# A fused attention and two-MoE kernel: squares to ScalarE, y of two chunks transposed on TensorE, and a new hand-written order of the lead and the first block

## Chip, cores and metric

The kernel runs on one NeuronCore of a Trainium2 chip. The metric is the device time of one execution in microseconds (us). The kernel before takes 1087.73 us in the median of three runs (1086.11, 1087.73 and 1088.6).

## What is computed

Three layers follow each other, all in float32 at the interface.

```python
# 1. attention-like recurrence, B, H, S, D = 4, 8, 768, 48
mag = sqrt(a_re**2 + a_im**2)
scale = minimum(mag, 0.999) / (mag + 1e-6)      # a is shortened to a magnitude below 1
for t in range(S):                              # per batch and head, state S is D x D, complex
    S = a[t][:, None] * S + outer(k[t], v[t])
    y[t] = q[t] @ real(S)
x = y as (B*S, H*D) = (3072, 384)
# 2. first MoE-like layer, w_in 384 x 2048, w_out 2048 x 384
h = x @ w_in;  x = (h * tanh(softplus(h))) @ w_out        # "mish"
# 3. second layer, w_a and w_b 384 x 1536, w_out 1536 x 384
out = ((x @ w_a) * (x @ w_b)) @ w_out
```

## The kernel before

The sequence is cut into chunks of 128 tokens: chunk c is sequence block j = c // 4 of batch b = c % 4, 24 chunks in all. Inside a chunk the recurrence becomes matrix products: decays are turned into logarithms and angles, summed along the tokens by a matmul with a triangular matrix, q and k are scaled and rotated by them, transposed on TensorE, multiplied with each other to scores, and the scores with v to y. What reaches a chunk from earlier blocks comes through a state matrix W per batch. The tokens of four chunks (one block, 512 tokens) then go through the first layer in 16 units of 128 hidden columns each, and after all blocks through the second layer in 12 units per block. The layers work on pairs of tensors (a high part and a low part in the TensorE format fp32r), three matmuls for each product; the second product of block 0 is done in plain fp32 instead.

The names of steps that matter below, with their lines:

- decay steps of a chunk: `sq` squares the real and imaginary parts (decay_1, L283: on VectorE in L285 for chunks 1 to 3, on ScalarE in L287 otherwise), `add` sums them (L291), `ln`, `ex`, `tan`, `ell` follow; `pl` and `pt` are the running sums on TensorE (L355); `red` reduces the angle on VectorE (L386 to L388); `sin` is the trigonometry on ScalarE; `rq` and `rk` rotate q and k (L433), `tq`, `tk` transpose them on TensorE (L452), `s` makes scores on TensorE (psc, L475), `cp` masks them into SBUF on VectorE (L481).
- y of a chunk: chunks 0 and 1 are named in BY_MEMORY (L487) and make y already transposed (py, L508); ScalarE makes a high part (yh, L521), VectorE a low part (yl, L526), both are stored to DRAM by SyncE (L533) and loaded again as the layer's input (xh, xl, L590). Chunks 2 and 3 make y with tokens on the partitions (pyt, L498), ScalarE copies it out (yt), TensorE transposes it (px, L586), ScalarE makes the high part xh (L592) and VectorE the low part xl (L598).
- state: `ou` is the outer product of k and v on TensorE (pu, L552), with the pads of k cleared first by GpSimd (L547); `st` makes the state W from it on VectorE (L569).
- weights of the first layer: `w.n` loads 768 KB, `da`, `dc`, `db` split it in three passes of VectorE (L172, L174, L176), `hi` on ScalarE and `lo` on GpSimd (L188) make the two parts.
- first layer, unit n: `h.n` is the first product (hps, L650), `mn` (L656, VectorE), `ma`, `mb` (ScalarE) and `pr` (L680, VectorE) make mish, `x.n` is the second product into one PSUM accumulator (x2ps, L706).

The order of all this is no loop: up to the 17th unit of block 0 a string of step names is executed one by one in `run` (L969 to L997), and `in_order` pins what each of the five engines gets in exactly that order. Everything behind the list is placed by a planner that spreads attention steps over slots between the layer's units. `close` in the list ends the SBUF pools of the first four chunks (end_lead, L954); `open` ends their PSUM pool and opens the accumulator x2ps in its place (end_first, L959), so the first x2ps matmul has to wait until all that was in that PSUM pool (pl, pt, pyt, px and pu of the first four chunks) is read out.

Of the kernel before, what the change touches and what calls it, by code (L numbers as in the profile page):

```python
# [21 lines left out]
def kernel(  # L22
# [14 lines left out]
    nc = tc.nc  # L37
# [26 lines left out]
    B, H, S, D = q.shape  # L64
# [153 lines left out]
    st = {}  # L218
# [740 lines left out]
    def end_first():  # L959
# [9 lines left out]
    run("""  # L969
            a0 sq0 add0 ln0 ex0 a3 sq3 add3 tan0 at0 pt0 ell0 pl0 ln3 ex3 w.1 da.1 dc.1 db.1 hi.1 lo.1 a1 sq1  # L970
            tan3 add1 ell3 ep0 red0 ln1 he0 qk0 sc0 a2 sq2 v0 ex1 ell1 pl1 w.2 da.2 w.3 add2 dc.2 sin0 rq0
            tq00 tq10 tan1 da.3 rk0 dc.3 ht0 db.2 ln2 a4 qk1 re0 ep1 ex2 at1 he1 at3 cq10 sq4 tk10 ck10 pt1
            db.3 tan2 cq00 at2 hi.3 tk00 ck00 lo.3 sc1 add4 ln4 ell2 pl3 s10 cp10 pt3 pl2 ep2 red3 red1 pt2
            red2 he2 s00 cp00 py0 ep3 ex4 tan4 at4 qk2 qk3 sc2 ell4 pl4 v3 cy4 ca4 vm4 a5 w.4 v1 w.5 sin1 rq1
            tq11 rk1 pt4 tk11 sc3 sin2 rq2 ep4 he4 em4 qk4 sq5 cq11 yt0 he3 add5 tq12 cq12 tk01 ck01 ck11 ln5
            ou0 tq01 cq01 ex5 sin3 ht3 v2 red4 ht4 gm4 re4 re3 v4 re1 xl0 da.4 rk2 da.5 s11 cp11 dc.4 tq02
            cq02 s01 tk02 ou1 cp01 ck02 ht1 tk12 ck12 dc.5 sin4 py1 rq3 tq13 cq13 sy0 yt1 rk3 db.5 hi.5 db.4
            s02 cp02 xl1 st0 gm5 tk13 tq03 ck13 tk03 s12 cp12 st1 io0 re2 lo.5 s13 cp13 cq03 ck03 s03 py2 yt2
            cp03 py3 ht2 px2 xh2 yt3 ou3 sc4 tan5 at5 ell5 rk4 tk04 ms4 ck04 w.6 sy1 vm5 da.6 rq4 xl2 dc.6 px3
            xh3 xl3 close cy5 w.7 ca5 da.7 dc.7 db.7 tk14 ck14 pl5 ep5 tq14 cq14 tq04 ou2 io1 h.0 h.1 st3 mn.0  # L980
            st2 open so.0 sl.0 so.1 em5 db.6 s14 cp14 mn.1 cq04 hi.7 lo.7 ma.0 mb.0 pr.0 pt5 red5 a6 he5 re5
            qk5 w.8 v5 s04 cp04 ma.1 sq6 mb.1 add6 ln6 ou4 ex6 h.2 da.8 mn.2 pr.1 so.2 ma.2 mb.2 tan6 sc5 dc.8
            ell6 pr.2 x.0 x.1 sl.1 py4 sd4 ht5 sin5 ms5 at6 h.3 rk5 rq5 mn.3 ma.3 mb.3 yt4 db.8 h.4 mn.4 ma.4
            mb.4 w.9 da.9 cy6 ca6 pr.3 xl4 dc.9 db.9 tq05 cq05 x.2 pt6 red6 st4 x.3 sl.2 vm6 hi.9 lo.9 gm6
            tk15 w.10 a7 qk6 tq15 sq7 ck15 h.5 tk05 pr.4 da.10 mn.5 cq15 s15 cp15 ck05 ma.5 pl6 ep6 add7 dc.10
            db.10 s05 cp05 em6 mb.5 pr.5 h.6 so.3 ou5 ln7 ex7 ht6 sin6 w.11 sc6 he6 da.11 ell7 sy4 re6 py5
            tan7 dc.11 sd5 st5 v6 vm7 gm7 ms6 x.4 x.5 sl.3 mn.6 yt5 xl5 at7 ma.6 db.11 hi.11 lo.11 pl7 ep7 cy7
            w.12 ca7 pt7 h.7 rq6 rk6 tk16 mb.6 pr.6 h.8 em7 mn.7 ma.7 mb.7 red7 da.12 he7 w.13 re7 x.6 mn.8
            da.13 ma.8 tq06 pr.7 x.7 so.4 sl.4 tk06 dc.13 db.13 hi.13 lo.13 ck16 tq16 h.9 dc.12 db.12 mb.8
            pr.8 qk7 mn.9 ht7 cq06 ms7 cq16 s16 sin7 sc7 rq7 cp16 w.14 da.14 a8 dc.14 h.10 mn.10 ck06 s06 cp06  # L990
            ma.9 x.8 ou6 w.15 da.15 mb.9 pr.9 db.14 rk7 ma.10 mb.10 sy5 py6 yt6 sd6 so.5 so.6 x.9 sl.5 tq17
            cq17 tk17 ck17 dc.15 pr.10 xl6 w.16 da.16 dc.16 db.16 tq07 sq8 db.15 tk07 h.11 ck07 h.12 add8
            mn.11 mn.12 cq07 s07 cp07 qk8 v7 ou7 s17 cp17 hi.15 lo.15 ma.11 mb.11 x.10 ln8 pr.11 ex8 ell8 ph8
            py7 sd7 st7 ma.12 mb.12 sy6 cy8 io4 yt7 io6 h.13 mn.13 x.11 sl.6 pd8 pr.12 pl8 tan8 xl7 ma.13
            mb.13 pr.13 h.14 mn.14 h.15 at8 ca8 qh8 qd8 ma.14 mb.14 x.12 x.13 mn.15 ma.15 mb.15 pr.14 pr.15 a9
            sy7 io5 io7 h.16 h.17 mn.16 mn.17 ma.16 mb.16 pr.16 ma.17 mb.17 x.14 x.15 pr.17 st6
    """)  # L997
    last, after_lead = in_order(first, (E.DVE, E.Activation, E.PE, E.Pool, E.SP)), traced()
    slot[0] = 50
# [249 lines left out]
```

## Time and profile before

| | us |
|---|---|
| median of three runs | 1087.73 |
| the profiled execution, its own time | 1088.15 |
| its span from the first to the last instruction | 1086.40 |
| TensorE busy | 1044.8 (96%) |
| VectorE busy | 653.2 (60%) |
| ScalarE busy | 609.2 (56%) |
| GpSimd busy | 230.3 (21%) |

So 1.75 us of the profiled execution lie outside its span. The page gives the core's mean granted TensorE clock as 0.996 of full speed. In its 40 slices TensorE is at 2 tenths in the first slice of 27 us and at 8 in the second; from then on it is at 9 or more up to the last slice, with 7. VectorE's slices go the other way: 7, 9, 8, 8, 8, 7 at the start and 2 to 4 at the end. Lines and names in the profile are those of the kernel's source; "x2ps<-gh,wout" reads: x2ps is written from gh and wout.

### The profile page before, as it was taken

What the parts mean: (1) busy time and instruction counts of PE and PEld (TensorE: products, weight loads), DVE (VectorE), ACT (ScalarE), POOL (GpSimd) and SP (SyncE); (2) the same over time, 40 slices, a digit from 0 to 9 for tenths busy, and PEclk for the clock granted to TensorE, in tenths of its full rate; (3) what the DMA queues carried; (4) which work ended last, traced back from release to release, by engine and by line L of the source; (5) the groups of instructions that cost most, each with busy time, mean ns of one, the idle gap of its engine ahead of it and who ended that gap; (6) DMA issues with size and microseconds to landing.
All of it is one profiled execution on the core that took longest, in us unless ns stands there. A gap on an engine that the chain in (4) does not pass through costs nothing.

```text
span 1086.4 us, 15900 instructions
## 1 busy us (share of the span) xinstructions
PE 1044.8 (96%) x6054; PEld 871.9 (80%) x6054; DVE 653.2 (60%) x1001; ACT 609.2 (56%) x963; POOL 230.3 (21%) x265
## 2 busy tenths in 40 slices
PE   2899999999999999999999999999999999999997
PEld 1676676788888888888877788888888888888886
DVE  7988875888777777677579998632322422422222
ACT  7968877898788887898767842221122222212211
POOL 3022323444344344333231123100000000000000
PEclk9999999999999999999999999999999999999999
DMA  9665653444443344333155366110100100100000
GB/s 217 140 172 128 168 133 102 119 94 101 101 91 68 67 96 85 84 96 80 30 169 180 124 220 215 45 51 1 30 30 1 59 1 1 44 1 1 30 1 32
DMA packets 206813, 92.50 MB, mean 85 GB/s; under 512 B 144973, under 2 KB 191114, under 8 KB 206730
## 3 DMA queue, kind: packets, MB, share of 16 engines
q1 hardware_dynamic: 205674, 91.20, 34.0%
q8 instruction: 50, 0.82, 0.3%
q10 hardware_dynamic: 1056, 0.21, 0.1%
q14 instruction: 33, 0.27, 0.1%
HBM read 73.23 MB, written 18.15 MB: 84 GB/s over the span
## 4 chain that ended last, share of the span: by engine, by line
PE 80%; DVE 8%; ACT 6%; issue 2%; DMA 2%; POOL 1%; SPq 0%; ACTq 0%; DVEq 0%; POOLq 0%
PE ops L790 14%; PE x2ps L706 14%; PE psa L765 14%; PE psb L765 14%; PE hps L650 13%; PE psc L475 3%; ACT m L59 3%; PE py L508 3%; PE pkT L452 2%; PE pqT L452 1%; PE pu L552 1%; ACT L54 1%; DMA a<-in_a_im_dram 1%; DVE wf L174 1%; PE pt L355 1%
## 5 line engine op out<-in xcount | busy, mean ns | idle before, releaser
L776 DVE TENSOR_TENSOR a_sb<-a_sb,psb 128x512 f32<-128x512 f32 x72 | 49.4, 686 | 225.8 <-PE psb L765 225.8
L59 ACT ACTIVATE m<-m 128x512 f32<-128x512 f32 x192 | 118.9, 632 | 60.2 <-DVE m L656 55.0
L59 ACT ACTIVATE a_sb<-psa 128x512 f32<-128x512 f32 x72 | 43.0, 598 | 163.5 <-PE psa L765 161.4
L59 ACT ACTIVATE ph<-a_sb 128x512 fp32r<-128x512 f32 x72 | 45.4, 631 | 154.8 <-DVE a_sb L776 154.8
L650 PE MATMUL hps<-xh,winh 128*128 128x512 f32 x288 | 117.1, 407 | 2.0 <-DVE m L683 1.3
L690 POOL TENSOR_TENSOR gl<-m,gh 128x512 fp32r<-128x512 f32 x64 | 83.6, 1307 | 156.5 <-DVE gh L689 133.1
L650 PE MATMUL hps<-xl,winh 128*128 128x512 f32 x288 | 113.5, 394 | 1.4 <-DVE wf L174 1.4
L650 PE MATMUL hps<-xh,winl 128*128 128x512 f32 x288 | 113.5, 394 | 0.0
L790 PE MATMUL ops<-woh,ph 128*128 128x384 f32 x288 | 97.2, 337 | 0.0
L790 PE MATMUL ops<-woh,pl 128*128 128x384 f32 x288 | 97.1, 337 | 0.0
L790 PE MATMUL ops<-wol,ph 128*128 128x384 f32 x288 | 96.7, 336 | 0.0
L706 PE MATMUL x2ps<-gl,wouth 128*128 128x512 f32 x240 | 94.6, 394 | 2.2 <-DVE gl L690 1.2
L706 PE MATMUL x2ps<-gh,wouth 128*128 128x512 f32 x240 | 93.9, 404 | 1.8 <-ACT gh L59 1.5
L706 PE MATMUL x2ps<-gh,woutl 128*128 128x512 f32 x240 | 93.9, 391 | 0.0
L683 DVE SCALAR_TENSOR_TENSOR m<-m,hps 128x512 f32<-128x512 f32 x80 | 54.6, 684 | 60.3 <-ACT m L59 59.9
L765 PE MATMUL psa<-xh,wal 128*128 128x512 f32 x216 | 85.2, 394 | 0.0
L765 PE MATMUL psa<-xl,wah 128*128 128x512 f32 x216 | 85.1, 394 | 0.0
L765 PE MATMUL psa<-xh,wah 128*128 128x512 f32 x216 | 84.3, 390 | 0.0
L765 PE MATMUL psb<-xh,wbh 128*128 128x512 f32 x216 | 84.2, 390 | 0.0
L765 PE MATMUL psb<-xh,wbl 128*128 128x512 f32 x216 | 84.2, 390 | 0.0
L765 PE MATMUL psb<-xl,wbh 128*128 128x512 f32 x216 | 84.2, 390 | 0.0
L778 DVE TENSOR_TENSOR pl<-a_sb,ph 128x512 fp32r<-128x512 f32 x72 | 52.0, 722 | 39.0 <-ACT ph L59 39.0
(169 smaller groups left out, 2324.5 us busy)
## 6 DMA issues: line engine op xcount, KB each, us to landing
wraw<-in_moe_w_out_dram SPq DMA_DIRECT2D x14, 768.0 KB
wraw<-in_moe_w_in_dram SPq DMA_DIRECT2D x8, 768.0 KB
a<-in_a_re_dram SPq DMA_DIRECT2D x24, 192.0 KB
q<-in_q_dram SPq DMA_DIRECT2D x24, 192.0 KB
k<-in_k_dram SPq DMA_DIRECT2D x24, 192.0 KB
v<-in_v_dram SPq DMA_DIRECT2D x24, 192.0 KB
x_d<-x2o SPq DMA_DIRECT2D x18, 256.0 KB
wraw<-in_moe_w_a_dram SPq DMA_DIRECT2D x6, 768.0 KB
```

The costliest lines, as they stand in the source:

```text
L59: x = nc.scalar.activation(**kw)
L452: nc.tensor.transpose(p[:, i, :], src[:, h].rearrange("p a d -> p (a d)") if c < B else own[:, h], ident)
L475: nc.tensor.matmul(p[:, i, :], lhsT=st["kT", c, hf][:, i, :], rhs=st["qT", c, hf][:, i, :], start=True, stop=True)
L508: nc.tensor.matmul(p[par * 64:(par + 1) * 64, i, :], lhsT=w[:, col:col + 64], rhs=x[:, first + par, :], start=(n == 0), stop=(n == len(ter ...
L650: nc.tensor.matmul(p, lhsT=w[:, kk, :], rhs=x[:, kk, :], start=(i == 0), stop=(i == len(ops) - 1))
L683: nc.vector.scalar_tensor_tensor(m, m, 2.5, p, ALU.subtract, ALU.mult)
L690: (nc.vector if on_act else nc.gpsimd).tensor_tensor(gl, m, gh.bitcast(F32), ALU.subtract)
L706: nc.tensor.matmul(x2ps[m], lhsT=w[:, ms], rhs=x, start=(f == 0 and i == 0), stop=(f == NF - 1 and i == len(terms) - 1),)
L765: nc.tensor.matmul(p, lhsT=w[:, kk, :], rhs=x[:, kk, :], start=(i == 0), stop=(i == len(ops) - 1))
L776: nc.vector.tensor_tensor(a_sb, a_sb, pb, ALU.mult)
L778: nc.vector.tensor_tensor(lo, a_sb, hi.bitcast(F32), ALU.subtract)
L790: nc.tensor.matmul(ops_t[t], lhsT=x[:, tsl], rhs=w, start=(f == 0 and i == 0), stop=(f == NF2 - 1 and i == 2),)
```

## The change

Four things are edited. The squares of chunks 1 to 3 go from VectorE to ScalarE. BY_MEMORY is empty, so that y of chunks 0 and 1 is made, copied, transposed and split as that of chunks 2 and 3 was. The pads of v and g of chunks 0 to 3 are cleared before the list begins, and the clearing of k's pads becomes a step of its own, `pk`. And the list is written anew in all its places.

```diff
     def decay_1(c):
-        if c in (1, 2, 3):
-            nc.vector.tensor_tensor(pair(c, "s", "qh", "a", "h"), st["a", c], st["a", c], ALU.mult)
-            return
         act(out=pair(c, "s", "qh", "a", "h"), in_=st["a", c], func=AF.Square)
...
-    BY_MEMORY = (0, 1)
+    BY_MEMORY = ()
...
+    def clear_kh(c):
+        nc.gpsimd.memset(st["kh_flat", c][:, 2 * H * D:], 0.0)
+
     def outer(c):
         if chunk(c)[0] == NC - 1:
             return
         vt = st["v", c]
-        if c < B:
-            nc.gpsimd.memset(st["kh_flat", c][:, 2 * H * D:], 0.0)
...
     first = traced()
+    for c in range(B):
+        clear_v(c)
+        clear_g(c)
     run("""
...
-            cp03 py3 ht2 px2 xh2 yt3 ou3 sc4 tan5 at5 ell5 rk4 tk04 ms4 ck04 w.6 sy1 vm5 da.6 rq4 xl2 dc.6 px3
-            xh3 xl3 close cy5 w.7 ca5 da.7 dc.7 db.7 tk14 ck14 pl5 ep5 tq14 cq14 tq04 ou2 io1 h.0 h.1 st3 mn.0
-            st2 open so.0 sl.0 so.1 em5 db.6 s14 cp14 mn.1 cq04 hi.7 lo.7 ma.0 mb.0 pr.0 pt5 red5 a6 he5 re5
-            qk5 w.8 v5 s04 cp04 ma.1 sq6 mb.1 add6 ln6 ou4 ex6 h.2 da.8 mn.2 pr.1 so.2 ma.2 mb.2 tan6 sc5 dc.8
-            ell6 pr.2 x.0 x.1 sl.1 py4 sd4 ht5 sin5 ms5 at6 h.3 rk5 rq5 mn.3 ma.3 mb.3 yt4 db.8 h.4 mn.4 ma.4
...
+            cq14 w.7 da.7 xl3 px2 xh2 xl2 pl5 ep5 em5 tk04 ck04 dc.7 db.7 hi.7 db.6 s14 h.0 pk3 lo.7 vm5 pk2
+            close mn.0 cp14 pt5 red5 qk5 re3 a6 sq6 add6 s04 cp04 h.1 mn.1 sc5 ma.0 mb.0 pr.0 he5 re5 w.8 ht5
+            w.9 ou4 ln6 ex6 tan6 ell6 da.8 ou1 py4 sd4 st4 ms5 gm6 ma.1 mb.1 pr.1 da.9 h.2 v5 cy6 re2 vm6 dc.8
+            dc.9 mn.2 db.8 db.9 at6 ca6 sin5 rq5 rk5 pl6 ep6 he6 yt4 ma.2 ou2 ou3 st3 xl4 st2 st1 open x.0
...
```

Three places of the order follow, each as it stands in one kernel. Lines of the changed kernel are lower by 2 or 3, except those ahead of decay_1.

TensorE's instructions around the first x2ps matmul, before (the last three of h.2, then x.0, then the first two of x.1):

```order
L650 MATMUL hps<-xh,winh_302 128x512
L650 MATMUL hps<-xl,winh_302 128x512
L650 MATMUL hps<-xh,winl_311 128x512
L706 MATMUL x2ps_933<-gh,wout_238 128x512 [waits DMAHW4_49,DMAHW1_49,DMAHW0_49]
L706 MATMUL x2ps_935<-gh,wout_238 128x512
L706 MATMUL x2ps_937<-gh,wout_238 128x512
L706 MATMUL x2ps_933<-gh,wout_238 128x512 [waits DVE_49]
L706 MATMUL x2ps_935<-gh,wout_238 128x512
```

The same place in the changed kernel (the last two of h.2, pl of chunk 6, the outer products of chunks 2 and 3, then x.0):

```order
L648 MATMUL hps<-xl,winh_387 128x512
L648 MATMUL hps<-xh,winl_389 128x512
L352 MATMUL pl<-size,csum 128x384 [waits DVE_49,PE_49]
L550 MATMUL pu<-v,kh 64x48 x15
L550 MATMUL pu<-v,kh 64x48 [waits Pool_49]
L550 MATMUL pu<-v,kh 64x48 x16
L704 MATMUL x2ps_964<-gh,wout_230 128x512 [waits DMAHW4_49,DMAHW3_49,DMAHW5_49,DMAHW2_49,DMAHW6_49,DMAHW0_49,DMAHW7_49,DVE_49,PE_49]
L704 MATMUL x2ps_966<-gh,wout_230 128x512
```

The outer products of chunks 2 and 3 (pu from kh, 16 matmuls each) now stand directly ahead of the first x2ps, and pl of chunk 6 ahead of them; the outer product of chunk 1 and y of chunk 4 stand some places further up, behind h.1. The first x2ps now waits for VectorE too, by the semaphore that its instruction W_130 (below) raises.

VectorE's instructions around the first mish step (m from hps), before. W_132 and W_131 are the states of batches 3 and 2; those of batches 0 and 1 are made earlier:

```order
L172 TENSOR_SCALAR wf_748<-wraw 128x768 [waits DMAHW1_49,Pool_49]
L174 SCALAR_TENSOR_TENSOR wf_748<-wraw,wf_748 128x768 [waits DVE_49]
L176 SCALAR_TENSOR_TENSOR wf_748<-wraw,wf_748 128x768 [waits DVE_49]
L569 TENSOR_TENSOR W_132<-pu,g 128x384 [waits DMAHW3_49]
L656 TENSOR_SCALAR m<-hps 128x512 [waits DMAHW6_49,DMAHW3_49,PE_49]
L569 TENSOR_TENSOR W_131<-pu,g 128x384
L176 SCALAR_TENSOR_TENSOR wout_729<-wraw,wout_729 128x768
```

In the changed kernel the first mish step stands as number 99 of VectorE's instructions. The last ones of the stretch that ends with W_130 are numbers 121 to 128:

```order
L176 SCALAR_TENSOR_TENSOR wf_877<-wraw,wf_877 128x768 [waits DVE_49]
L324 SCALAR_TENSOR_TENSOR a<-size,a 1x384 [waits DMAHW1_49,Activation_49]
L430 TENSOR_TENSOR qhp<-q,a 128x16x48 [waits Activation_49]
L430 TENSOR_TENSOR khp<-k,a 128x16x48
L567 TENSOR_TENSOR W_132<-pu,g 128x384 [waits DMAHW6_49,PE_49]
L523 TENSOR_TENSOR yl<-py,yh 128x512 [waits Activation_49]
L567 TENSOR_TENSOR W_131<-pu,g 128x384 [waits DMAHW3_49,DMAHW2_49]
L567 TENSOR_TENSOR W_130<-pu,g 128x384
```

Three of the four state steps have moved behind the first mish step, and W_130 is the 30th instruction counted from that step on, both counted. Of these 30 are, beside the three state steps: 3 first mish steps (L654), 2 products (L678), 2 masks (L478), 3 of a reduced angle (L383 to L385), 6 decode passes (two of L172, four of L174 and L176), 2 rotations (L430), 1 low part of y (L523), and 8 short ones of decay, scaling and state.

VectorE's first instructions that work on data, before:

```order
L291 TENSOR_TENSOR qhp<-qhp 128x384 [waits Activation_49]
L285 TENSOR_TENSOR s<-a 128x768 [waits DMAHW3_49,DMAHW2_49]
L291 TENSOR_TENSOR s<-s 128x384 [waits DVE_49]
L306 TENSOR_TENSOR a<-a,r 128x384 [waits DMAHW0_49,Activation_49]
L312 TENSOR_SCALAR qhp<-qhp 128x384
```

And in the changed kernel:

```order
L288 TENSOR_TENSOR qhp<-qhp 128x384 [waits Activation_49]
L288 TENSOR_TENSOR s<-s 128x384 [waits Activation_49]
L303 TENSOR_TENSOR a<-a,r 128x384 [waits DMAHW0_49,Activation_49]
L309 TENSOR_SCALAR qhp<-qhp 128x384 [waits DVE_49]
L844 CAST csum_r<-csum 128x128 [waits Pool_49]
```

The square is gone from VectorE, and the second sum waits for ScalarE in its stead.

## Rows read from the trace of the kernel before

**Rows 1.** Windows of the whole core: busy time by engine, matmul clock, DMA share.
```profile
core 0: us, PE busy (x) PEld busy (x) DVE busy (x) ACT busy (x) POOL busy (x), PEclk, DMA share, GB/s
20.00:40.00 20.00, 12.86 (x60) 8.52 (x60) 19.69 (x35) 17.24 (x28) 2.29 (x10) 1.00 1.05 193
60.00:80.00 20.00, 17.92 (x175) 14.76 (x175) 15.91 (x24) 13.37 (x23) 4.50 (x5) 0.91 0.77 204
80.00:180.00 100.00, 100.00 (x574) 67.40 (x574) 74.28 (x113) 81.22 (x121) 26.03 (x24) 1.00 0.52 127
```

**Rows 2.** Chain of waits, 55 to 100 us: start us, us, what.
```profile
61.74 5.35 DMA wraw<-in_moe_w_in_dram
...
69.62 5.74 PE hps L650 x17
...
75.37 0.89 PE psc L475 x8
76.26 0.65 PE pt L355 x2
...
77.79 1.07 PE pu L552 x32
78.86 2.27 PE hps L650 x9
81.13 3.00 PE x2ps L706 x7
...
86.28 1.90 PE py L508 x32
```

**Rows 3.** TensorE's waits, 60 to 186 us: us in total, times, longest.
```profile
PE hps L650 <- DMA xl<-yt_dl: 0.7, 1, 0.7
```

**Rows 4.** Window from VectorE's first sum to the first mish step, columns as Rows 1.
```profile
5.85:72.48 66.63, 45.69 (x374) 35.12 (x375) 63.15 (x102) 52.79 (x83) 10.25 (x23) 0.96 0.88 182
```

**Rows 5.** VectorE's timeline: start us, duration us, instruction, idle time before it.
```profile
7.08 0.96 DVE L285 TENSOR_TENSOR s<-a 128x768 f32<-128x768 f32 x1 [0.67 <-DMA a<-in_a_im_dram]
...
14.29 2.05 DVE L312 TENSOR_SCALAR s<-s 128x384 f32<-128x384 f32 x1
...
20.10 0.35 DVE L312 TENSOR_SCALAR s<-s 128x384 f32<-128x384 f32 x1
...
30.31 2.05 DVE L313 SCALAR_TENSOR_TENSOR size<-r,s 128x384 f32<-128x384 f32 x1
...
63.38 0.56 DVE L172 TENSOR_SCALAR wout<-wraw 128x768 uint32<-128x768 uint32 x1 [1.19 <-DMA wraw<-in_moe_w_out_dram]
...
64.72 0.55 DVE L598 TENSOR_TENSOR xl<-px,xh 128x384 fp32r<-128x384 f32 x1
...
68.78 2.46 DVE L176 SCALAR_TENSOR_TENSOR wf<-wraw,wf 128x768 uint32<-128x768 uint32 x1
...
72.48 0.69 DVE L656 TENSOR_SCALAR m<-hps 128x512 f32<-128x512 f32 x1 [0.77 <-PE hps L650]
```

**Rows 6.** GpSimd's timeline beside the long VectorE step.
```profile
13.84 2.19 POOL L188 TENSOR_TENSOR winl<-wf,winh 128x768 fp32r<-128x768 f32 x1 [6.94 <-ACT winh L59]
```

**Rows 7.** ScalarE's timeline: its first square.
```profile
4.97 0.84 ACT L59 ACTIVATE qhp<-a 128x768 f32<-128x768 f32 x1 [2.37 <-DMA a<-in_a_im_dram]
```

**Rows 8.** VectorE's groups, 72.48 to 100 us: busy us, mean ns, idle before.
```profile
L656 DVE TENSOR_SCALAR m<-hps 128x512 f32<-128x512 f32 x5 | 3.4, 684 | 0.9 <-PE hps L650 0.8
L176 DVE SCALAR_TENSOR_TENSOR wout<-wraw,wout 128x768 uint32<-128x768 uint32 x2 | 1.9, 946 | 0.0
L481 DVE COPY_PREDICATED am<-csum,psc 128x512 f32<-128x512 int32 x2 | 1.5, 735 | 1.8 <-PE psc L475 1.8
L388 DVE TENSOR_SCALAR a<-a 128x384 uint32<-128x384 uint32 x2 | 0.7, 361 | 0.1
L526 DVE TENSOR_TENSOR yl<-py,yh 128x512 fp32r<-128x512 f32 x1 | 0.7, 684 | 0.0
L569 DVE TENSOR_TENSOR W<-pu,g 128x384 f32<-128x384 f32 x1 | 0.5, 547 | 0.0
```

**Rows 9.** TensorE's timeline: y of chunks by both ways, and the first late transpose.
```profile
38.01 1.09 PE L508 MATMUL py<-am,v 128*64 128x128 f32 x16 [3.09 <-DVE am L481]
...
59.55 1.95 PE L498 MATMUL pyt<-v,before_x 128*128 128x48 f32 x16
...
61.34 0.51 PE L586 MATMUL px<-ident,yt 128*128 128x128 f32 x3
...
194.32 0.66 PE L452 MATMUL pqT<-ident,qhp 128*128 128x128 f32 x4 [0.42 <-DVE qhp L433]
```

**Rows 10.** Windows of TensorE alone: us, PE busy (matmuls), granted clock, DMA share.
```profile
66.95:69.62 2.67, 0.63 (x7) 1.00 0.99 204
...
70.70:74.10 3.40, 3.40 (x10) 0.50 0.77 123
74.10:80.00 5.90, 5.90 (x61) 1.00 0.56 163
```

More of the change, by code (lines that the diff above doesn't have):

```diff
@@ L919, in run @@
             "sq": decay_1, "add": decay_sum, "ln": decay_ln, "ex": decay_3, "tan": tangent, "ell": size,
-            "pl": sum_ell, "ep": lambda c: decay_exp(c, c < B), "em": decay_inverse, "vm": clear_v, "gm": clear_g, "he": hand_end, "sc": scale_qk, "at": angle, "cy": fetch_turn,
+            "pl": sum_ell, "ep": lambda c: decay_exp(c, c < B), "em": decay_inverse, "vm": clear_v, "gm": clear_g, "pk": clear_kh, "he": hand_end, "sc": scale_qk, "at": angle, "cy": fetch_turn,
             "ca": add_turn, "pt": turned, "red": reduce_angle, "ht": hand_turn, "sin": trig, "ms": clear_pads,
@@ L968 @@
     first = traced()
+    for c in range(B):
+        clear_v(c)
+        clear_g(c)
     run("""
[L970 to L978, printed above, removed]
@@ L984 @@
[L984 to L993, printed above, removed]
@@ L994 @@
-            py7 sd7 st7 ma.12 mb.12 sy6 cy8 io4 yt7 io6 h.13 mn.13 x.11 sl.6 pd8 pr.12 pl8 tan8 xl7 ma.13
-            mb.13 pr.13 h.14 mn.14 h.15 at8 ca8 qh8 qd8 ma.14 mb.14 x.12 x.13 mn.15 ma.15 mb.15 pr.14 pr.15 a9
-            sy7 io5 io7 h.16 h.17 mn.16 mn.17 ma.16 mb.16 pr.16 ma.17 mb.17 x.14 x.15 pr.17 st6
+            a0 a1 sq0 add0 ln0 sq1 add1 ex0 tan0 ell0 ln1 ex1 ell1 pl1 at0 tan1 at1 ep1 a2 sq2 pl0 ep0 w.1
+            da.1 dc.1 db.1 hi.1 lo.1 w.2 da.2 dc.2 he1 he0 add2 ln2 qk1 sc1 pt0 red0 a3 sq3 add3 pt1 red1 qk0
@@ new lines @@
+            sc0 ex2 ell2 pl2 tan2 ln3 ex3 ell3 sin0 rq0 tq10 tq00 tan3 rk0 tk00 pk0 sin1 rk1 pk1 rq1 at2 ep2
+            v3 vm4 w.3 da.3 a4 sq4 ht0 add4 cq10 cq00 dc.3 ln4 ck00 tk11 pt2 pl3 tq11 ck11 ex4 re0 v1 qk2 red2
+            sc2 ell4 db.3 db.2 tan4 ep3 s00 cp00 tk10 at3 pt3 red3 hi.3 lo.3 he2 v4 re1 ck10 tk01 v0 at4 cq11
+            he3 qk3 v2 a5 cy4 sin2 sq5 sc3 rq2 s10 cp10 sin3 s11 ou0 ht1 tq01 pl4 ep4 rk2 cp11 ca4 em4 st0
+            add5 rk3 gm4 gm5 w.4 cq01 ht3 ck01 tk12 ck12 tq12 py0 tk02 ht2 yt0 cq12 rq3 tq13 w.5 qk4 sc4 da.4
@@ new lines @@
+            da.5 dc.4 tk13 s01 cp01 ln5 cq13 px0 ck13 ck02 xh0 pt4 tq03 cq03 red4 xl0 dc.5 tk03 ex5 ck03 db.4
+            py1 yt1 tq02 cq02 he4 re4 db.5 hi.5 s13 cp13 s03 px1 xh1 cp03 ell5 ms4 lo.5 s12 s02 tan5 at5 ht4
+            sin4 py3 yt3 cp02 cp12 py2 yt2 xl1 px3 xh3 rk4 tk14 ck14 rq4 tq04 cq04 cy5 ca5 w.6 da.6 dc.6 tq14
+            cq14 w.7 da.7 xl3 px2 xh2 xl2 pl5 ep5 em5 tk04 ck04 dc.7 db.7 hi.7 db.6 s14 h.0 pk3 lo.7 vm5 pk2
+            close mn.0 cp14 pt5 red5 qk5 re3 a6 sq6 add6 s04 cp04 h.1 mn.1 sc5 ma.0 mb.0 pr.0 he5 re5 w.8 ht5
@@ new lines @@
+            w.9 ou4 ln6 ex6 tan6 ell6 da.8 ou1 py4 sd4 st4 ms5 gm6 ma.1 mb.1 pr.1 da.9 h.2 v5 cy6 re2 vm6 dc.8
+            dc.9 mn.2 db.8 db.9 at6 ca6 sin5 rq5 rk5 pl6 ep6 he6 yt4 ma.2 ou2 ou3 st3 xl4 st2 st1 open x.0
+            so.0 sl.0 pt6 red6 w.10 w.11 re6 hi.9 em6 so.1 so.2 so.3 lo.9 mb.2 x.1 h.3 mn.3 pr.2 tq05 cq05
+            tk05 ck05 ma.3 mb.3 tq15 cq15 tk15 ck15 da.10 dc.10 x.2 h.4 s05 ht6 da.11 db.10 dc.11 db.11 pr.3
+            ou5 a7 sq7 add7 so.4 ln7 ex7 hi.11 mn.4 ma.4 mb.4 cp05 tan7 s15 cp15 h.5 mn.5 qk6 sc6 ell7 ma.5
@@ new lines @@
+            mb.5 sl.1 x.3 sl.2 pr.4 ms6 lo.11 sy4 py5 yt5 sd5 pr.5 st5 gm7 v6 at7 sin6 h.6 mn.6 ma.6 x.4 pl7
+            x.5 sl.3 w.12 da.12 dc.12 db.12 xl5 h.7 w.13 da.13 cy7 ca7 pt7 ep7 he7 em7 w.14 re7 rq6 tq16 dc.13
+            mb.6 pr.6 x.6 tq06 ms7 vm7 mn.7 ma.7 mb.7 rk6 qk7 db.13 hi.13 cq16 lo.13 h.8 red7 ht7 da.14 pr.7
+            x.7 sl.4 tk16 mn.8 ma.8 mb.8 dc.14 db.14 tk06 h.9 pr.8 mn.9 ck06 ck16 cq06 s16 cp16 s06 cp06 w.15
+            da.15 sy5 w.16 da.16 sc7 a8 io4 v7 dc.16 h.10 ou6 py6 x.8 ma.9 sin7 rq7 mn.10 rk7 db.16 sd6 mb.9
@@ new lines @@
+            pr.9 ma.10 yt6 dc.15 tk07 ck07 tk17 ck17 h.11 a9 xl6 sy6 io6 so.5 x.9 sl.5 mb.10 mn.11 ma.11 tq17
+            cq17 pr.10 db.15 mb.11 pr.11 hi.15 so.6 lo.15 tq07 sq8 cq07 h.12 mn.12 add8 ma.12 ln8 s17 cp17
+            x.10 s07 cp07 h.13 mn.13 ma.13 py7 yt7 xl7 x.11 sl.6 mb.12 mb.13 pr.12 pr.13 ou7 ex8 ell8 ph8 h.14
+            mn.14 h.15 mn.15 ma.14 mb.14 sd7 pr.14 ma.15 mb.15 x.12 sy7 io5 io7 qk8 h.16 x.13 mn.16 ma.16
+            mb.16 pr.15 pd8 pr.16 st7 st6 h.17 mn.17 ma.17 tan8 x.14 x.15 mb.17 pr.17 pl8 cy8 at8 ca8 qh8 qd8
```

## The prediction

> **What bounds the kernel now.** First the windows of the whole core. From 80 to 180 us TensorE is busy in all 100 of 100 us at full clock, with VectorE at 74 and ScalarE at 81 [rows 1]. So behind 80 us TensorE is the bound, and what is lost or won ahead of that is carried to the end. From 20 to 40 us it is the reverse: VectorE 19.69 of 20, TensorE 12.86 [rows 1]. From 5.85 us, its first sum, to 72.48 us, the first mish step, VectorE is busy 63.15 of 66.63 us [rows 4]; its idle time there is 3.48 us. The lead is VectorE's.
>
> Then the chain of waits, for how the lead ends: a weight load, its decode on VectorE, TensorE's hps from 69.62 on, scores, sums, outer products, and the first x2ps matmul at 81.13 us [rows 2]. From 69.62 TensorE does not stop again. So the time of the first x2ps, call it X, measures the lead, if one also counts what TensorE has done by then.
>
> **What the change moves, and the point of balance.** Two pieces stand ahead of X in the new order that stood behind it: y of chunk 4, 1.90 us, and a running sum like the one of 0.65 us [rows 2]. The outer products that it moves were ahead of X and stay there. With the same work behind, the new kernel breaks even when X is at 81.13 + 1.90 + 0.65 = 83.7 us; each us above is lost, each below is won.
>
> **Y of chunks 0 and 1.** TensorE now makes it in 16 matmuls of 1.95 us and 3 transposes of 0.51, instead of 16 of 1.09 [rows 9]: 1.4 us for a chunk by these durations, 2.7 for both. It stands ahead of h.0, where TensorE waits for VectorE (12.86 of 20), so I cost it at nothing; uncovered it is 2.7. What it replaces is a round trip through DRAM; TensorE waited 0.7 us for its load [rows 3], and that is all it can give back. SyncE's 12 fewer transfers free a queue that no other row waits for: nothing. On VectorE the low part becomes 0.55 instead of 0.68 [rows 5, 8].
>
> **The squares.** VectorE loses three of 0.96 us [rows 5]; ScalarE, 52.79 busy of 66.63 [rows 4], gains three of 0.84 [rows 7]. VectorE's second sum now waits for ScalarE instead, so not all of the 2.9 need come in: at most one such wait of 0.84 for each, 2.5 together, which lies inside the ends below. The Trainium skill says in "Trainium Architecture — The Big Picture", section "The five engines, in one table", that ScalarE is not for simple arithmetic and that VectorE is up to about 3 times faster per element on trn2. By that rule three squares on ScalarE would take 8.6 us against 2.9, and the lead would grow by up to 5.8 where ScalarE is awaited; the rows, 0.84 against 0.96 for the same 768 columns, speak against it, and I take the rows.
>
> **Pads.** GpSimd's clearing is early and in time; I cost it at nothing. If a pad were late, its reader on TensorE would wait for some tenths.
>
> **VectorE up to the first mish step.** By the order, the work ahead of it loses three squares (2.9), two low parts of y (1.4) and two state steps of 0.55 (1.1), and gains two low parts of x (1.1) and one decode pass (0.95) [rows 5, 8]: 3.3 us by durations. Instructions of VectorE overlap by some 0.08 us each in the timeline, so it is 2.9 from start to start. With every stall left as it is, the first mish step would begin at 72.48 - 2.9 = 69.6 us. Two waits and a stretch sit in steps that change place: 1.19 for a weight, 0.77 for TensorE, and 1.5 in a decode pass of 2.46 us [rows 5] instead of 0.95 [rows 8]. Without these 3.5 us it is 66.1. I take the middle, 67.8, since nothing in the rows says which stay, and keep both ends.
>
> **VectorE from there to X.** This is the term that decides. In the new order x2ps waits for W_130, the 30th instruction from the first mish step on. By kinds [rows 5, 8]: 3 mish steps, 2 products and 1 low part at 0.68 (4.1), 2 masks at 0.73 (1.5), 4 decode passes and 2 rotations at 0.95 (5.7), 2 first passes at 0.56 (1.1), 3 state steps at 0.55 (1.6), 3 of the angle at 0.55, 0.56 and 0.36 (1.5), 8 short ones at 0.35 to 0.56 (4.1). That is 19.6 us by durations and, less 30 times 0.08, 17.2 from start to start. Before, the last state step followed the first mish step directly. TensorE cannot cover this: from h.0 on it has three units of 2.27, four outer products of 1.07, one half of scores of 0.89, two sums of 0.65 and y of 1.90 [rows 2], 15.2 us in all, while VectorE needs the 17.2 and, ahead of the first mish step, three more decode passes (2.6). So it idles some 5 us in front of X.
>
> X comes to 67.8 + 17.2 = 85.0 us, 1.3 above balance. The ends are 66.1 + 17.2 = 83.3 (0.4 won) and 69.6 + 17.2 = 86.8 (3.1 lost).
>
> **The clock.** At 66.95 to 69.62 us TensorE was busy 0.63 of 2.67 us, and soon after, from 70.70 to 74.10, its granted clock was 0.50, that is 1.2 GHz instead of 2.4, with 10 matmuls in 3.40 us where some 15 would have gone; after that it was 1.00 again [rows 10]. An idle stretch of 5 us ahead of X is longer than that, so I expect another such dip behind X, where TensorE is the bound: half of 3.4 us, 1.7 lost. Ends: 0 (no dip) and 3.4 (two).
>
> **Behind X.** The two kernels run the same units and the same planner. The rotation of chunk 8 kept TensorE waiting by 0.42 us before [rows 9]; the new list leaves its angle later, so this wait may grow to 2. I take no change.
>
> **Sum.** 1.3 + 1.7 = 3.0 us. The profiled execution took 1088.15 us (span 1086.40, 1.75 outside), 0.4 above the median of 1087.73. So 1091.15 by that execution, and **1090.7 us** against the median. Over 0.2%, 2.2 us, is what a measurement here can tell from no change.
>
> **Rivals.** *The lead is shorter (faster).* In VectorE's lead lie three instructions stretched from 0.35, 0.56 and 0.95 us to 2.05, 2.05 and 2.46, 4.7 us in all [rows 5], the first two while or near GpSimd subtracts a low weight part (13.84 to 16.03) [rows 6]; with the 3.48 idle that makes 8.2. If the new order puts other work beside GpSimd and leaves few gaps, the first mish step comes at 72.48 - 2.9 - 8.2 = 61.4 at best, X at 78.6, 5.1 won: 1082.6. From X below 81.5 without a dip it is faster by over 2.2; the middle of that is some 1084.5. For it: VectorE is bound in the lead, and the change unloads it. Against it: three subtractions stay in the lead. The Trainium skill, "SBUF — State Buffer", section "Who interferes with whom", says that VectorE and GpSimd exclude each other for whole instructions on a shared port pair, whoever issues first. The trace agrees, with 2.05 against 0.35 beside one of 2.19. By that rule a stretch vanishes only where VectorE does something outside those forms at the time. Chance 0.27.
>
> *It evens out (same).* No dip, and X between 82 and 85.5: 1086.5 to 1089.5, near 1088. For it: the clock fell after sparse work, and TensorE does have short work ahead of X that might hold it. It is also the case in which the change does little of what it says, since the round trip was hidden but for 0.7 us. Chance 0.25.
>
> *Slower than forecast.* Everything at the upper end: X at 86.8, a dip, and chunk 8 later by 2: 3.1 + 1.7 + 2 = 6.8, 1094.5. It shares 0.48 with my forecast, of which it has 0.15.
>
> **How the numbers follow.** Slower by over 0.2% 0.48, within 0.2% 0.25, faster 0.27. The range takes in the forecast, the even case, the middle of the faster one and nearly all of the slow one: 1083.5 to 1094.5. The slower case's own range is 1090 to 1094.5.
>
> **What would show it.** In the new profile: VectorE's squares gone; the first mish step at 66 to 70 us; a wait of x2ps for VectorE's W of 3 to 7 us, ending at 83 to 87; granted clock at 0.50 for some 3 us soon behind it; then TensorE full to 180 us. If x2ps waits under 2 us for VectorE, or begins before 81.5, my reading of the order is wrong in its price and the kernel is faster. If the first mish step comes after 70, ScalarE's chain in the lead, which I cost at nothing, is the late one.

## The result and the profile after

The changed kernel takes 1097.48 us in the median of four runs (1096.02 to 1098.93) where the kernel before takes 1087.63 (four runs): 1.0094 times as long, with a 95% interval of 1.008 to 1.0109, 9.9 us slower. The forecast had the direction right, and the wait in front of the first x2ps and the clock behind it about right; but its range ended at 1094.5, and it put nothing on the end of the list. The profiled execution took 1098.33 us, with a span of 1096.6.

The windows of the changed kernel, columns as in [rows 1] (busy time and count of each engine, clock, DMA):

```profile
20.00:40.00 20.00, 14.17 (x96) 10.33 (x96) 19.61 (x36) 18.12 (x30) 2.11 (x2) 0.76 1.08 228
60.00:80.00 20.00, 16.67 (x214) 13.55 (x212) 19.00 (x32) 18.21 (x27) 3.11 (x7) 1.00 0.57 132
80.00:100.00 20.00, 16.44 (x54) 9.77 (x55) 11.09 (x18) 11.08 (x18) 5.44 (x3) 0.83 0.60 153
...
180.00:200.00 20.00, 14.26 (x53) 10.98 (x52) 13.66 (x23) 17.72 (x25) 8.53 (x13) 0.84 0.59 177
```

The last of these windows in the kernel before, for comparison:

```profile
180.00:200.00 20.00, 18.24 (x90) 14.38 (x89) 16.06 (x24) 18.42 (x31) 13.22 (x16) 1.00 0.62 157
```

VectorE is still the full engine up to 80 us. From 20 to 40 us the clock is lower too (0.76, before 1.00), but VectorE is the bound there. New are two windows in which TensorE is neither full nor at full clock: 80 to 100 and 180 to 200. TensorE's waits in the list (us in total, times, longest) name both:

```profile
PE x2ps L704 <- issue: 6.5, 1, 6.5
PE hps L648 <- DVE m L681: 5.4, 1, 5.4
```

The first is the predicted wait for W_130 (the releaser is not resolved, "issue", but VectorE's last state step ends 83.46 and x2ps starts 83.56). The chain of waits shows it between its neighbours: start, us, what.

```profile
62.63 2.12 PE hps L648 x8
...
75.05 2.03 PE pu L550 x64
77.07 6.49 issue
83.56 4.87 PE x2ps L704 x6
88.44 0.65 PE pt L352 x2
89.08 2.57 PE x2ps L704 x6
```

The same six x2ps matmuls take 4.87 us behind the wait and 2.57 in the next unit: 2.3 us lost behind the wait, some 2.0 of them by the lower clock alone, as the expectations below count it. TensorE's windows (us, busy, granted clock, DMA) show it behind both waits:

```profile
77.00:83.50 6.50, 0.05 (x2) 0.80 0.55 182
83.50:88.40 4.90, 4.84 (x7) 0.57 0.30 80
88.40:92.00 3.60, 3.60 (x12) 1.00 0.09 16
189.90:195.30 5.40, 0.09 (x1) 0.84 0.44 130
195.30:200.30 5.00, 4.94 (x12) 0.50 0.48 157
```

For accounts of the whole, TensorE's timeline gives the start of the same work in each kernel: the first hps, the first x2ps, and the first hps of units 18 and 24 (the list ends about unit 18; between units 18 and 24 both kernels do the same 212 matmuls, and behind unit 24 the two keep their distance to within 0.3 us).

| start, us | before | changed | later by |
|---|---|---|---|
| first hps | 67.78 | 61.77 | -6.0 |
| first x2ps | 80.97 | 83.56 | 2.6 |
| hps of unit 18 | 177.90 | 180.63 | 2.7 |
| hps of unit 24 | 213.81 | 223.05 | 9.2 |
| last ops | 1079.72 | 1088.90 | 9.2 |

So the lead was 6 us shorter up to the first hps, and 8.6 us went in front of x2ps: 2.55 on the y and the sum moved ahead, the rest by the wait. At 2.6 later it stood at the point of balance. The clock then took 2.3. And between units 18 and 24, at the end of the list, 6.5 us went that the forecast did not have.

What happened there is on ScalarE, in order (timeline: start, us, instruction, idle before and its releaser):

```profile
178.76 0.60 ACT L59 ACTIVATE x2o<-x2ps 128x512 f32<-128x512 f32 x1 [1.27 <-PE x2ps L704]
181.51 0.60 ACT L59 ACTIVATE x2o<-x2ps 128x512 f32<-128x512 f32 x1 [2.15 <-DMA x_d<-x2o]
182.00 0.72 ACT L59 ACTIVATE m<-m,bias_fifth 128x512 f32<-128x512 f32 x1
182.75 0.63 ACT L59 ACTIVATE m<-m 128x512 f32<-128x512 f32 x1
183.40 1.28 ACT L54 ACT_TABLE_LOAD   x1
184.69 0.53 ACT L59 ACTIVATE a<-a 128x384 f32<-128x384 f32 x1
185.24 1.28 ACT L54 ACT_TABLE_LOAD   x1
...
192.26 1.13 ACT L59 ACTIVATE m<-m 128x512 f32<-128x512 f32 x2
```

The second evacuation of the block's x2ps (x2o, the copy of the finished accumulator out of PSUM) waits 2.15 us for the first one's store to land. The kernel before stands idle at the same place too, 2.85 us. But here the second half of unit 17's mish is behind it in ScalarE's order (the new list has `x.15 mb.17`, the old `mb.17 x.14 x.15`), and behind that the angle of chunk 8 with two table loads, which in the kernel before ScalarE does between units 13 and 14 (from 160.59 us), four units earlier. VectorE's order then passes the delay on: two steps of that angle (L324, L344) stand ahead of unit 18's first mish step (L654), which starts at 187.53, 6.9 us behind the unit's first hps (180.63); before it was 2.8 (180.65 behind 177.90). Unit 18's mish comes out of ScalarE only at 192.9; VectorE is then in a weight's decode (its split into parts), and TensorE waits (VectorE's timeline, then TensorE's):

```profile
185.25 1.09 DVE L324 SCALAR_TENSOR_TENSOR a<-size,a 1x384 f32<-1x384 f32 x1 [0.69 <-ACT a L59]
187.05 0.56 DVE L344 SCALAR_TENSOR_TENSOR sl<-a,sh 128x384 fp32r<-128x384 f32 x1 [0.71 <-POOL v L245]
187.53 0.68 DVE L654 TENSOR_SCALAR m<-hps 128x512 f32<-128x512 f32 x1
...
193.28 0.96 DVE L176 SCALAR_TENSOR_TENSOR wf<-wraw,wf 128x768 uint32<-128x768 uint32 x1
194.15 0.55 DVE L303 TENSOR_TENSOR a<-a,khp 128x384 f32<-128x384 f32 x1
194.62 0.68 DVE L681 SCALAR_TENSOR_TENSOR m<-m,hps 128x512 f32<-128x512 f32 x1
```

```profile
195.36 0.79 PE L648 MATMUL hps<-xh,winh 128*128 128x512 f32 x1 [5.36 <-DVE m L681]
```

In the kernel before the same matmul waited 1.35 us. So 4.0 of the 6.5 us are this wait. The eleven matmuls behind it take 4.64 us (195.36 to 200.00) against 2.54 before (188.41 to 190.95), 2.1 more at the lower clock; the last 0.4 I did not trace.

### The profile page after: what moved, and what is told of

Read it like the earlier page. It is cut to its first block, busy times and chain, and to the rows that moved or that the text cites. A ratio compares the mean times of both kernels' runs of the same rounds, so it can differ in the third digit from the quotient of the medians.

```text
span 1096.6 us, 15887 instructions
## 1 busy us (share of the span) xinstructions
PE 1048.2 (96%) x6060; PEld 875.1 (80%) x6060; DVE 645.6 (59%) x998; ACT 610.3 (56%) x966; POOL 229.3 (21%) x265
## 4 chain that ended last, share of the span: by engine, by line
PE 78%; DVE 8%; ACT 7%; issue 3%; DMA 3%; POOL 1%; SPq 0%; DVEq 0%; ACTq 0%; POOLq 0%
PE ops L788 14%; PE x2ps L704 14%; PE psa L763 13%; PE psb L763 13%; PE hps L648 12%; ACT m L59 3%; PE py L505 3%; PE psc L472 3%; PE pkT L449 1%; PE pu L550 1%; PE pqT L449 1%; DMA a<-in_a_im_dram 1%; ACT L54 1%; DMA wraw<-in_moe_w_in_dram 1%; DVE m L681 1%
## 5 line engine op out<-in xcount | busy, mean ns | idle before, releaser
L654 DVE TENSOR_SCALAR m<-hps 128x512 f32<-128x512 f32 x96 | 65.6, 684 | 21.7 <-PE hps L648 21.6
```

The lines of the kernel that those rows point to most:

```text
L654: nc.vector.tensor_scalar(m, p, 20.0, None, ALU.min)
```

## The experiments

Theory: the order makes the loss, by three things: the wait in front of x2ps, the tail's wait, and the clock behind each. Rival: the parts (y on TensorE, squares on ScalarE) are dear. All ratios are to the kernel before, run on the same chip. Differences between two changed kernels are those of their medians; the medians of the kernel before beside them lie from 1087.6 to 1088.5 us, so such a difference is good to about 1 us.

**The state steps early.**

```diff
-            h.2 v5 cy6 re2 vm6 ... ou2 ou3 st3 xl4 st2 st1 open x.0
+            pt5 red5 qk5 re3 re2 a6 ... ou1 ou2 ou3 py4 sd4 st1 st2 st3 st4 ... xl4 open x.0
```

> The changed kernel, with the outer products of chunks 1 to 3 and their state steps moved up behind y of chunk 4, so that the first x2ps no longer waits for VectorE's W_130. Theory (the order makes waits): the 6.5 us idle stretch in front of x2ps (77.07 to 83.56) goes, x2ps starts near 77, and the half-clock stretch behind it (2.0 us lost) goes too: 6 to 8.5 us faster than the changed kernel, some 1089 to 1091.5, with the 5.4 us wait near 190 still there. Rival (the parts are dear: TensorE's extra 2.7 us and ScalarE's squares): x2ps is held by something else at once, and the time stays within 3 us of 1097.5.

Measured: 1092.23 us, ratio 1.0034 (1.0021 to 1.0048), 5.3 us faster than the changed kernel (6.5 by the ratios). The first x2ps starts at 76.50, 7.1 us earlier than in the changed kernel, and the half-clock stretch is gone, which should give 2.3 more; but unit 18 is only 7.0 us earlier: the next piece, the sum of angles of chunk 6, now waits for VectorE (chain, start, us, what):

```profile
79.79 0.87 DVE wf L176
80.66 0.47 DVE a L324
...
81.17 0.91 PE pt L352 x2
82.08 2.57 PE x2ps L704 x6
```

The tail is as it was (from unit 18 to 24 42.4 us, in the changed kernel 42.4, before 35.9). The theory's mechanism is shown, wait and half clock in front of and behind x2ps are gone; the gain is at or just under the lower end of its 6 to 8.5. The rival is out.

**One step of the tail.**

```diff
-            mn.17 ma.17 tan8 x.14 x.15 mb.17 pr.17 pl8 cy8 at8 ca8 qh8 qd8
+            mn.17 ma.17 mb.17 tan8 x.14 x.15 pr.17 pl8 cy8 at8 ca8 qh8 qd8
```

> The changed kernel, with one step moved at the end of the list: ScalarE does the second half of unit 17's mish ahead of the evacuation of the block's x2ps instead of behind it. Theory: the product of unit 17 comes near 179 instead of 183.4, ScalarE is 1 to 2 us earlier behind it, and the 5.4 us wait near 190 shrinks to 3 to 4.5: 1 to 2.5 us faster, some 1095 to 1096.5. Rival (the wait is made by the angle of chunk 8 and its two table loads, which still stand at the end): no change within 1 us.

Measured: 1097.81 us, ratio 1.0085 (1.0068 to 1.0102). The wait shrank to 3.8 us and units 18 to 24 to 40.8, 1.6 less, but in this profile the first x2ps came at 87.63 instead of 83.56, with the same instructions ahead of it. That execution was the slowest of its four (1101.35 us). No gain of 1 us can be told from such a spread, so the time decides neither for the theory nor for the rival; the step is tried again below.

**The whole tail.**

```diff
-            ou7 ex8 ell8 ph8 h.14 mn.14 h.15 mn.15 ... pr.15 pd8 pr.16 ...
-            mn.17 ma.17 tan8 x.14 x.15 mb.17 pr.17 pl8 cy8 at8 ca8 qh8 qd8
+            ou7 ex8 ell8 ph8 pd8 pl8 tan8 cy8 h.14 mn.14 h.15 at8 ca8 qh8 qd8 mn.15 ... pr.15 pr.16 ...
+            mn.17 ma.17 mb.17 x.14 x.15 pr.17
```

> The changed kernel, with that step moved and also the angle and the running sum of chunk 8 put ahead of the last units, where the kernel before has them. Theory: the wait near 190 falls from 5.4 to the 1.4 us of the kernel before, and the half-clock stretch at 195 to 200 (2.0 us lost) goes: 4 to 6 us faster than the changed kernel, 1091.5 to 1093.5; x2ps still starts at 83.6. Rival (what is lost there comes from TensorE being later than before, not from the order): the wait stays above 4 us and the time within 2 us of 1097.5.

Measured: 1095.45 us, ratio 1.0069 (1.0052 to 1.0086), 2 us faster than the changed kernel. The wait at 190 fell from 5.4 to 0.2 us, units 18 to 24 to 34.8, though TensorE came there 3.8 us later than in the changed kernel, so the rival is out. The time fell short of the theory's 4 to 6: the sum of chunk 8 waited in its new place, and the lead was 1.5 us late in the profile (x2ps at 85.10). TensorE's waits:

```profile
PE x2ps L704 <- issue: 6.6, 1, 6.6
PE pl L352 <- POOL sh L338: 2.4, 1, 2.4
```

**Both edits.** The two diffs above together.

> Both edits together: states early, and the tail as in the kernel before. Theory: the gains add, 10 to 14.5 us: 1083 to 1087.5, faster than both kernels. Rival: TensorE reaches the tail earlier than ScalarE can follow, and half of the lead's gain is given back there: 1088 to 1091.

Measured: 1088.25 us, ratio 0.9998 (0.9986 to 1.001): level with the kernel before, short of the theory's lowest gain, and where the rival had it, but not for the rival's reason: units 18 to 24 take 34.8 us. The two new waits, 1.9 and 2.4 us, are both there, and this time each has a half-clock stretch behind it: from 80 to 84 us the granted clock was

```profile
80.00:84.00 4.00, 2.93 (x4) 0.67 0.80 233
```

against, in the kernel with the states early, with the same wait 0.1 us later,

```profile
80.00:84.00 4.00, 2.83 (x7) 1.00 0.72 228
```

**The squares alone.** The kernel before without its branch for chunks 1 to 3 in decay_1.

> The kernel before, with its own order, and only the squares of chunks 1 to 3 on ScalarE. Theory (the order makes the loss): VectorE's second sum waits for ScalarE, but the lead is relieved by up to 2.9 us; between 2 us faster and 1 us slower than the kernel before. Rival (ScalarE's squares are dear in the lead): 2 to 6 us slower.

Measured: 1087.18 us, ratio 0.9993 (0.9983 to 1.0003): no change. The rival is out for the squares.

**Y of chunks 0 and 1 alone.** The kernel before with BY_MEMORY empty.

```diff
-            v4 re1 xl0 da.4 ... tq13 cq13 sy0 yt1 ... cp02 xl1 ... st1 io0 re2 ... w.6 sy1 vm5 ... ou2 io1 h.0
+            v4 re1 px0 xh0 xl0 da.4 ... tq13 cq13 yt1 ... cp02 px1 xh1 xl1 ... st1 re2 ... w.6 vm5 ... ou2 h.0
```

> The kernel before, with its own order, and only y of chunks 0 and 1 made, transposed and split like that of chunks 2 and 3, with the steps put where the loads were awaited. Theory: TensorE's 2.1 to 2.7 us more lie ahead of h.0 where it waits for VectorE, and the wait of 0.7 for the load goes: within 1.5 us of the kernel before. Rival (the work on TensorE is not covered): 2 to 3 us slower.

Measured: 1094.32 us, ratio 1.0054 (1.0036 to 1.0071), 6 us slower: the rival's direction at twice its price, and not by its mechanism. VectorE's waits, 30 to 80 us, say why; the first is not there in the kernel before, and the second is 1.8:

```profile
DVE xl L598 <- ACT xh L59: 5.4, 2, 5.1
DVE am L481 <- PE psc L475: 3.7, 2, 3.0
```

The low part stood in VectorE's order 5 us ahead of its input. That is the place I gave it, so it was tried again, with the transposes earlier:

```diff
-            ou0 tq01 cq01 ... db.5 hi.5 db.4
+            ou0 px0 xh0 tq01 cq01 ... db.5 hi.5 px1 xh1 db.4
```

> The kernel before with y of chunks 0 and 1 on TensorE again, but with the transpose and the high part put earlier than VectorE's low part, so that VectorE does not stand still for them as it did for 5.4 us in the first try. Theory (its place was dear, not the work): within 2 us of the kernel before. Rival (the work is dear in this order wherever it stands): again 4 us or more slower.

Measured: 1089.04 us, ratio 1.0006 (0.9996 to 1.0016). With the same work on TensorE, and VectorE busy 16.6 of the 20 us from 40 on instead of the first try's 14.8 (before: 19.9), no difference to the kernel before can be told. The rival is out for y too; its place in the order decides what it costs. The pads have no run of their own.

**Filling the wait.**

```diff
+    def refill(c):
+        for h in range(H):
+            for i in range(2):
+                col = (2 * h + i) * D
+                nc.tensor.matmul(st["pu", c][i * 64:(i + 1) * 64, h, :], lhsT=st["kh_flat", c][:, col:col + 64],
+                                 rhs=st["v", c][:, h * D:(h + 1) * D], start=True, stop=True)
...
-            ma.2 ou2 ou3 st3 xl4 st2 st1 open x.0
+            ma.2 ou2 ou3 fl1 fl1 fl1 fl1 st3 xl4 st2 st1 open x.0
```

> The changed kernel, with the outer product of chunk 1 made four more times, into the same place, in the stretch in which TensorE waits in front of x2ps (4.3 of some 6.5 us filled with work that changes nothing). Theory (the idle stretch lets the clock fall): x2ps starts where it did, the granted clock behind it stays at 1.00, and the 2.0 us that the half-clock stretch cost come back: 1 to 2.5 us faster than the changed kernel. Rival (the clock falls for the kind of work behind, or at random): a half-clock stretch is still there and the time is that of the changed kernel, or later by what x2ps starts later.

Measured: 1098.24 us, ratio 1.0108 (1.0086 to 1.0129): nothing came back. The wait was 2.3 us, and still the clock fell behind it:

```profile
83.00:84.30 1.30, 0.00 (x0) 1.00 1.04 405
84.30:88.00 3.70, 3.69 (x6) 0.67 0.33 78
```

So 4.3 us of these matmuls did not keep it, with 2.3 us left idle. What would have kept it stays open.

**The waits mended.** Both edits, and the two sums moved behind work that is ready; with the second sum the angle steps of chunk 8 move back by one or two units as well.

```diff
-            so.0 sl.0 pt6 red6 w.10 ... x.1 h.3 mn.3 pr.2
+            so.0 sl.0 w.10 ... x.1 h.3 pt6 red6 mn.3 pr.2
...
+            ph8 h.14 mn.14 h.15 mn.15 ma.14 mb.14 tan8 sd7 pr.14 pd8 ma.15 mb.15 x.12 pl8 ... qk8 cy8 at8 h.16 ca8 x.13 mn.16 qh8 qd8
+            ... mn.17 ma.17 mb.17 x.14 x.15 pr.17
```

> The kernel with both edits, mended where its trace shows two new waits: the running sum of angles of chunk 6 goes behind h.3 instead of in front of x.1 (it waited 1.9 us for VectorE), and the running sum of chunk 8 goes behind x.12 instead of in front of h.14 (it waited 2.4 us for GpSimd). Theory: both waits and the two half-clock stretches behind them (1.8 and 1.7 us) go, some 4 to 7 us: 1081 to 1084.5, clearly faster than the kernel before. Rival: they come back elsewhere, because VectorE or ScalarE is the late one: 1086 to 1089.

Measured: 1085.29 us, ratio 0.9982 (0.9973 to 0.9992): faster than both kernels, 12.2 us under the changed one and 2.7 under the one before, just between the theory's range and the rival's. The profiled execution is the slowest of its ten (1087.43 us). TensorE's waits, and its clock from 77 us on:

```profile
PE pqT L449 <- DVE qhp L430: 2.3, 3, 1.4
PE hps L648 <- DVE m L681: 1.4, 1, 1.4
PE pqT L449 <- ACT qT L59: 1.2, 1, 1.2
PE hps L648 <- DVE gh L678: 0.7, 1, 0.7
```

```profile
77.00:80.00 3.00, 3.00 (x10) 1.00 0.02 6
80.00:84.00 4.00, 4.00 (x13) 1.00 0.42 113
84.00:88.00 4.00, 2.76 (x17) 1.00 0.84 284
```

Its first x2ps starts at 77.79, and units 18 to 24 take 35.91 us, exactly as before the change. The rival has a part in it: the first x2ps is 5.7 us ahead of balance (80.97 and the 2.55 moved ahead), but unit 18 only 2.5 us ahead of the kernel before (175.39 against 177.90). Of the 3.2 us lost on the way, two waits in the list above make 1.9, the 1.2 for ScalarE's qT and the 0.7 for VectorE's gh, and the rest is not traced. Three parts were undone on it, one each.

**Its tail's step put back** (`x.14 x.15 mb.17 pr.17`).

> The mended kernel, with the second half of unit 17's mish on ScalarE behind the evacuation of the block's x2ps again, as in the changed kernel. Theory (this step alone makes part of the late tail): the wait near 190 grows by 1 to 3 us and the kernel is 1 to 4 us slower. Rival (only the late angle of chunk 8 made the wait): within 1 us of the mended kernel.

Measured: 1087.56 us, ratio 0.9996 (0.9985 to 1.0008), 2.3 us slower than the mended kernel by the medians; by the ratios it is 1.5, and their intervals overlap, so the trace has to show it. The wait there is 2.8 instead of 1.4 us and the window from 180 to 200 has a clock of 0.91: units 18 to 24 take 38.7 us against 35.9. This step alone is part of the tail's loss, by its wait and by the clock behind it.

**Its squares put back on VectorE.**

> The mended kernel, with the squares of chunks 1 to 3 on VectorE again. Theory: VectorE is the bound of the lead, h.0 comes 1.5 to 2.9 us later and the kernel is as much slower. Rival (ScalarE is as late as VectorE there, so that the move gave nothing, as in the kernel before): within 1 us of the mended kernel.

Measured: 1088.6 us, ratio 1.0004 (0.9995 to 1.0014), 3.3 us slower than the mended kernel (2.4 by the ratios, whose intervals do not meet). The first hps comes 2.8 us later (66.28 against 63.48), near the price of three squares of 0.95. This fits VectorE as what the lead waits for in this order; but the first hps of kernels with one and the same lead lies between 61.77 and 65.72 in single profiles, so the price is the runs', not the profile's.

**Its y of chunks 0 and 1 through memory again.**

```diff
-            ... yt0 ... px0 ... xh0 ... xl0 ... px1 xh1 ... yt2 xl1 px3
+            ... yt0 ... xl0 sy0 io0 ... xl1 sy1 io1 ... yt2 px3
```

> The mended kernel, with y of chunks 0 and 1 sent through memory again. Theory: TensorE saves 2.1 to 2.7 us in front of h.0, where it waits for VectorE anyway: no change beyond 1 us, or up to 3 us slower if the load comes after h.0 could begin. Rival (TensorE is the bound of the new lead): 1.5 to 2.7 us faster.

Measured: 1094.76 us, ratio 1.0063 (1.0043 to 1.0082), 9.5 us slower than the mended kernel, far more than either theory. The load now stands right behind its own store on SyncE's queue, and the queue stands with it: the store of chunk 1's low part lands 2.19 us later, then go the load and, behind it, the small store of an angle, and ScalarE waits for that one (ScalarE's waits, 40 to 75 us, and the chain):

```profile
ACT a L59 <- DMA turn_d<-a: 6.1, 1, 6.1
```

```profile
57.28 0.44 SPq L530
...
57.76 2.19 DMA yt_dl<-yl
...
60.01 0.38 SPq L588
...
60.44 2.22 DMA turn_d<-a
...
62.69 1.03 ACT a L59 x2
```

A list that spaces stores and loads was not tried on the mended kernel, so the 9.5 us are the price of this placement; what y on TensorE is worth in the new order is not measured.

## Why the forecast missed

The sum was 1.3 for the lead, 1.7 for the clock and 0 behind X, 3.0 us; it measured 9.9.

- **Point of balance, 83.7.** As an account it holds: at 83.56 with 2.55 us of work moved ahead, the lead is level. "Each below is won" does not: of the mended kernel's 5.7 us, 2.5 were left at unit 18.
- **VectorE up to the first mish step, 66.1 to 69.6, taken 67.8.** It came at 65.22, just below the lower end. The first rival's mechanism came in: three weight subtractions ran on GpSimd (16.88, 35.12, 54.99), and VectorE had no instruction over 1.1 us in the lead, where before it had three of 2.05 to 2.46 [rows 5]. The row of GpSimd in the prediction goes with the first of these three only; the trace has a subtraction beside each (13.84, 30.04 and 68.17). In the changed kernel the steps of VectorE beside the subtractions mostly read PSUM tiles (pt, psc, px), and the one that only has the angle's own tile in SBUF (L385 at 18.02) took 1.03 us instead of 0.36. Against the rival, the second sum waited 1.65 us for ScalarE where I allowed 0.84.
- **VectorE from there to W_130, 17.2.** 18.2 us (65.22 to 83.46). Price and place of the wait were about right: 6.5 us against "some 5".
- **X at 85.0.** 83.56 in this profile; that it came so near is in part luck, since the first of its two parts was 2.6 too long and the second 1.0 too short. It was 85.10 and 87.63 in two kernels with the same lead. The lead's spread between executions is as large as the whole term.
- **The clock, 1.7.** 2.3 us behind X. Right in kind, and it happened a second time at 195 us (2.1 us), which was not in the sum as such.
- **Y, squares, pads, SyncE at nothing.** Borne out in the order of the kernel before for the squares (0.9993) and for y where it is well placed (1.0006); for pads and SyncE no run tells. On the mended order putting the squares back on VectorE cost 3.3 us. ScalarE's squares take 0.83 us in the changed kernel too, against VectorE's 0.96 before [rows 5]. The Trainium skill ("Trainium Architecture — The Big Picture", "The five engines, in one table") says that VectorE is up to about 3 times faster per element than ScalarE on trn2; the traces show nothing of that for this shape.
- **"It evens out", 1086.5 to 1089.5.** By the sum's own terms X at 82 gives 1086.0; nothing hangs on it.
- **"Behind X ... I take no change".** This is the step that failed: 6.5 us, units 18 to 24, of which 4.0 are one wait of TensorE for unit 18's mish and 2.1 the clock behind it. My ground was that both kernels run the same units and the same planner; beyond that I looked only at VectorE's rotation of chunk 8, with a row that showed a wait of 0.42, and bounded it at 2. I did not read ScalarE's order there, where one step behind an evacuation and the two table loads of an angle, and behind these the angle's steps on VectorE, make unit 18's mish late. The swap of that step alone took 1.6 us out of the stretch, and undone on the mended kernel it cost 2.3; with the angle moved too the stretch takes 34.8 to 35.9 us, as before.

The table adds it up: 0.0 for the lead's balance, 2.3 for the first clock stretch, 0.4 up to unit 18 that I did not trace, and 6.5 at the tail give 9.2, the difference of the last matmuls. The 0.7 between that and the medians is inside the runs' spread.

## What to carry to other kernels

An order pinned by hand is only as good as its worst in-order neighbour: for each matmul that opens a pool, read which engine's last reader it waits for, and count what stands ahead of that reader in its queue; a state step of 0.5 us, standing 30th, held TensorE for 6.5 us. Read the end of a hand-written list on every engine, not only on the bound one: there the evacuation waits for a store, and all behind it in that engine's order waits too. When a change adds many edits at once, put waits back one by one: here squares and y cost nothing in the old order, all edits together lost 9.9 us, and the same edits with the order's waits mended ended 2.7 us ahead of the kernel before.

## What the runs showed of the hardware

The granted clock does not fall after every wait of the same length. A wait of 1.9 us, at 79 to 81, left it at 1.00 with the states early, and with both edits it was 0.67 over the 4 us around the wait's end (0.50 from 81.4 to 84.7), with the same instructions around it. One of 2.4 us, for the sum of chunk 8, left it at 1.00 with the tail early and was followed by 3.3 us at half clock with both edits (0.50 from 159.9 to 163.2), 1.7 us lost. Behind waits of 2.3 us (the filled one) and 2.8 us (the tail's step put back) it fell too, and behind the longer ones of these traces, 3.8 to 7.3 us, each time. So a wait's price on TensorE was its length and, often but not surely, some 2 us more.

A load queued directly behind the store that it reads holds SyncE's whole queue until the store has landed (2.06 and 2.19 us here), and the bill of 6.1 us was paid by ScalarE, which takes part in neither.
